# One group of a fused attention and two-layer kernel: its first dense layer by seven products throughout, in a new order of all operations

## The chip, the cores and the metric

The kernel runs on one core of a Trainium2 chip. The metric is device time in microseconds, lower is better. Five engines work side by side, each through its own queue in order: TensorE (PE; PEld are its weight loads), VectorE (DVE), ScalarE (ACT), GpSimd (POOL) and SyncE (SP), which issues DMAs. They wait for each other by semaphores.

## The reference

Attention without a softmax feeds two dense layers:

```
scores = q @ k^T / sqrt(64);  attn = max(scores, 0)^2 / 448
x = (attn @ v), heads side by side: 3584 tokens x 768
h = x @ w_in        (768 x 2048)
g = h * sigmoid(1.702 h)
out = g @ w_out     (2048 x 768)
```

There are 8 batches, 12 heads, 448 positions and 64 dimensions per head. Inputs and output are fp32; the kernel computes in fp16 with fp32 accumulation.

## The kernel before

**Attention.** There are 24 units `u`: a batch and four of its heads. For unit `u` and each of seven blocks `j`, `scores` (word `s`, line 150) gives two tiles of 128x448 by four matmuls of 64x64 weights. `relu` (`r`, lines 161 on VectorE and 163 on ScalarE) takes each out of PSUM, `square` (`x`, line 88 on VectorE or GpSimd, 169 on ScalarE) squares both, and `attn_v` (`a`, line 181) multiplies by `v`, 28 matmuls. `xt_evac` (`e`) brings the result out as columns of `x^T` for a token group.

**Groups.** The tokens form eight groups `g` of 384 and 512 tokens in turn (`gblk = [6, 8] * 4`). Group 1 has 512. The tiles are `xe` and `xo` (x of even and odd groups), `ge` and `go` (the activations).

**First layer.** A group's h has 16 feature blocks of 128. It can be made in two ways. Plainly: `m1` (word `f`, line 228), three words of two matmuls for a block, then gelu (`g`, line 214) from PSUM into a fp32 tile `gf` and `widen` (`v`, line 217), which scales it to fp16 in `ge` or `go`. Or by a unit `i` of four feature blocks at once, with seven products instead of eight over halves of weights, features and tokens: `unit_product` (word `u`, seven words of six matmuls of half the columns, line 203) into two PSUM banks, with `unit_snap` (`t`, three copies out of the first bank), `unit_add` (`b`, three additions of the second bank to a copy), and gelu and widen of four quarters. It uses sums of weights (`S`, of `win` into `winS`) and of x (`T`), made by VectorE once for a unit or a group. There are five `gf` buffers.

**Second layer.** Pairs of 128-token tiles are multiplied by seven products too: `pair_product` (`p`, line 203, eight matmuls), with `A` (sums of activations), `W` (sums of `wout` into `wT`), `h` (`pair_snap`), `l` (`pair_last`). A group of 384 tokens has one tile over, done by `single` (`i`, evacuated by `n`). `o` and `q` store.

**Loads.** `jk`, `jq`, `V` (k, q, v of a unit), `jwa`, `jwb` (halves of a `win` block) and `jo` (a quarter of `wout`) are DMAs with a cast, issued by GpSimd, and so in one queue with its widenings. `Lk`, `Lq` are plain fp32 loads by SyncE, cast by `K` and `Q` on any engine and transposed by `Rk`, `Rq` (DMA) or, for the first six units, `tk`, `tq` on TensorE with `ek`, `eq`. `G3` makes SyncE wait until `win` block 3 has landed. `I` makes the identity matrix, `z` are matmuls on zeros.

**The order.** One list of words, written out by hand in the file, is gone through from first to last; each word issues its operation on its engine, so an engine's queue is the words for it in that order. A word is name, numbers, `:engine` (a, d or p for ScalarE, VectorE, GpSimd) and `@` PSUM banks. `u1.3.2` is group 1, unit 3, product 2 (counted from 0). Before the change group 1 makes its blocks 0 to 7 with `m1` and its units 2 and 3 by products; groups 2 to 7 are by products, group 0 by `m1`.

Of the kernel before, what the change touches and what calls it, by code (L numbers as in the profile page):

```python
# [15 lines left out]
def kernel(  # L16
# [406 lines left out]
    with tc.manual_schedule():  # L423
# [35 lines left out]
        def zeros(e, p, n):  # L459
# [8 lines left out]
            "jq1 z13@0 Lk0 I K0:d tk0@1 ek0 z1 Lq0 Q0:a tq0@2 tq1@3 jk1 eq0 s0.1@4.5 jwb2 jk2 "  # L468
            "s0.6@6.7 s0.4@0.1 r0.4.0:d r0.6.0 tk1@2 ek1 jq2 jq3 eq1 s0.3@6.0 r0.1.1 r0.4.1 "
            "r0.1.0 x0.1 s0.0@5.2 r0.0.0 s0.2@1.4 r0.2.0:d r0.3.1:d r0.3.0 s0.5@3.5 r0.6.1 "  # L470
            "s1.1@6.1 r0.2.1 r0.0.1:d s1.2@7.0 s1.5@4.2 x0.0 r0.5.0 r1.1.1 r1.2.1 jk3 x0.4 "
            "r0.5.1:d tq2@3 r1.2.0 x0.2 x0.6:a x0.5 x0.3 V0 r1.5.1 s1.0@1.0 x1.2 tk2@7 r1.5.0:d "
            "r1.0.0 ek2 tk3@5 r1.0.1 jwa0 s1.3@2.1 eq2 r1.1.0 x1.1:a V2 a0@0.6 V1 x1.5:a r1.3.1 "
            "s1.4@4.7 ek3 r1.3.0 jq4 jwb0 s2.1@3.5 r1.4.1 e0.0.1 s2.2@1.2 r1.4.0:d jk4 e0.0.0 "
            "jwa2 s1.6@4.7 x1.3 r1.6.1:d r2.1.0 r2.2.1 tq3@3 r2.2.0 e0.1.0 x1.4 r1.6.0 x1.6 "
            "r2.1.1 x1.0:p s2.6@2.1 jwa1 x2.2 s2.0@7.0 r2.0.1 r2.0.0 a1@4.5 r2.6.1 jwb1 e0.1.1:a "
            "e1.0.0:a s2.5@0.7 s2.3@1.6 r2.3.0 r2.3.1 e1.1.0:a x2.1 eq3 r2.6.0:d e1.0.1:a "
            "s2.4@3.2 r2.5.0:d r2.4.0:d r2.4.1:d jk5 f0.3.0@1 r2.5.1:d f0.2.0@0 x2.0:p tq4@6 eq4 "
            "tk4@4 s3.3@3.2 x2.6:p x2.3:a e1.1.1:a x2.4:p s3.2@7.5 x2.5:a jq5 r3.2.1:d r3.3.1:d "
            "r3.3.0 r3.2.0 f0.3.1 V3 ek4 f0.2.1 f0.0.0@6 s3.0@5.3 a2@2.7 e2.0.0 r3.0.0 S2.1 "  # L480
            "r3.0.1 x3.0:a e2.0.1:a s3.1@4.5 r3.1.0 f0.1.0@3 f0.0.1 f0.1.1 f0.1.2 e2.1.0:a g0.1 "
            "f0.0.2 V4 V5 jwb3 f0.2.2 x3.2 jwa3 g0.0 r3.1.1:d g0.2 f0.3.2 g0.3 x3.3 e2.1.1 "
            "s3.4@4.2 s3.5@5.3 r3.4.1:d s3.6@6.7 f0.8.0@0 f0.8.1 f0.4.0@1 G3 v0.1 r3.5.1:d r3.5.0 "
            "r3.4.0 x3.4 x3.5 x3.1 f0.8.2 f0.4.1 f0.4.2 r3.6.1 g0.8 s4.1@2.5 r3.6.0 v0.3 r4.1.1:d "
            "s4.3@3.4 r4.1.0 s4.2@7.0 r4.2.1 g0.4 f0.6.0@6 f0.6.1 f0.6.2 r4.2.0:d x3.6 tq5@2 "
            "tk5@5 r4.3.0 r4.3.1 x4.3 g0.6 x4.2:a x4.1 ek5 s4.0@0.7 a3@1.3 r4.0.1 r4.0.0 v0.0 "
            "s4.6@4.6 s4.4@7.5 jo0.0 eq5 f0.10.0@0 r4.4.0:d f0.10.1 f0.10.2 x4.0 v0.8 e3.0.0:a "
            "r4.6.1:d r4.4.1 f0.7.0@2 s5.4@1.7 e3.0.1:a s4.5@5.3 r4.6.0 g0.10 s5.1@4.6 v0.10 "
            "r4.5.0 f0.5.0@0 f0.5.1 f0.5.2 x4.6 f0.11.0@5 f0.11.1 f0.11.2 v0.6 f0.7.1 r4.5.1 "
            "r5.4.1 r5.1.0:d r5.1.1:d g0.5 x4.5:a v0.5 f0.7.2 r5.4.0:d s5.0@4.3 x4.4 s5.2@7.6 "  # L490
            "a4@0.1 r5.0.0:d r5.0.1:d g0.7 g0.11 jo0.1 v0.11 s5.6@2.5 r5.2.1 r5.2.0 s5.5@4.6 "
            "s5.3@3.7 r5.6.0:d e4.0.1:a f0.9.0@1 r5.3.1:d r5.3.0 r5.5.1:d v0.7 S0.1 r5.6.1:d "
            "f0.15.0@2 f0.15.1 r5.5.0 f0.14.0@3 x5.6 f1.1.0@7 jo1.1 f0.14.1 x5.5 v0.4 x5.1:a "
            "f0.9.1 v0.2 S3.1 jo1.0 f0.9.2 g0.9 v0.9 f0.13.0@4 f0.13.1 f0.12.0@6 f0.12.1 f1.3.0@5 "
            "e4.0.0:a S2.2 x5.4 Lq6 f0.15.2 Lk6 x5.0:a x5.3:a S2.3 S1.1 x5.2 f1.7.0@1 f0.14.2 "
            "g0.14 f0.12.2 g0.15 g0.12 S3.2 f1.7.1 f0.13.2 f1.5.0@0 Q6:d f1.0.0@3 f1.1.1 S2.4 "
            "g0.13 v0.13 a5@2.6 v0.15 e5.0.0 K6 e5.0.1:a Lk7 v0.14 S1.2 f1.0.1 f1.5.1 T1.1 "
            "f1.4.0@4 T1.2 v0.12 f1.7.2 S3.3 T1.4 W2.1 W0.1 f1.5.2 g1.7 v1.7 f1.6.0@2 A0.0.1@0 "
            "Lq8 g1.5 W3.1 f1.4.1 f1.4.2 g1.4 W2.2 f1.0.2 g1.0 Rk6 Rq6 v1.5 v1.0 f1.6.1 f1.3.1 "
            "u1.2.0@6 f1.2.0@1 t1.2.0 f1.1.2 W1.1 f1.3.2 K7 Rk7 u1.3.0@0 u1.2.1@4 g1.3 g1.1 v1.1 "  # L500
            "v1.3 Q8:a v1.4 f1.6.2 f1.2.1 f1.2.2 g1.2 v1.2 p0.0.0@3 h0.0.0 V8 b1.2.1 t1.3.0:d "
            "u1.3.2 u1.2.2 u1.2.3 Lk8 V6 W2.4 W0.2 T1.3 W2.3 g1.2.1 g1.6 t1.2.2 K8:p s6.0@5.7 "
            "s6.2@1.2 v1.2.1 r6.0.0 W1.2 u1.2.4 W3.2 r6.2.1:d r6.0.1 r6.2.0 t1.2.4 x6.0:a W3.3 "
            "u1.3.1@5 p0.0.1@2 W3.4 b1.3.1 A0.0.2@1 Lq7 s6.1@7.1 u1.2.5 b1.2.3 r6.1.1 r6.1.0:d "
            "l0.0.1 u1.3.3 u1.2.6 s6.3@1.7 W0.4 x6.1:a p0.0.2 W1.3 b1.2.6 Rq8 g1.2.3 r6.3.0:d "
            "t1.3.2 s6.5@4.1 A0.0.4 h0.0.2:d r6.3.1 u1.3.4 W0.3 v1.2.3 p0.0.3 Q7:a v1.6 r6.5.0 "
            "s6.6@7.4 Lq9 Q9 r6.5.1 g1.3.1 g1.2.5 t1.3.4 x6.2:a S3.4 A0.0.3 x6.5:a r6.6.0 W1.4 "
            "v1.3.1 b1.3.3 x6.3 V7 s6.4@1.6 r6.4.0 p0.0.4 u1.3.6 h0.0.4:d u1.3.5 Rq7 r6.6.1 "
            "l0.0.3 r6.4.1:d b1.3.6 p0.0.5 g1.2.6 g1.3.5 s7.4@7.1 s7.0@4.6 g1.3.6 g1.3.3 v1.3.3 "
            "l0.0.5:a v1.3.6 x6.6 s7.2@5.0 r7.2.0 Lk9 x6.4 r7.4.1:d r7.4.0 p0.0.6 r7.2.1 r7.0.0:d "  # L510
            "Rk8 K9:p r7.0.1:d l0.0.6 v1.2.6 x7.0:a s7.1@3.1 r7.1.1 r7.1.0:d a6@5.4 e6.0.0 "
            "e6.0.1:a e6.1.1 Lk11 e6.1.0 s7.5@7.6 s7.3@0.2 r7.5.1:d p1.0.0@3 A0.2.5@1 r7.5.0 x7.1 "
            "r7.3.0 s8.0@1.4 x7.4 s7.6@5.7 r7.6.1:d r8.0.0:d s8.1@0.6 v1.2.5 v1.3.5 r7.3.1 x7.3:a "
            "i0.2.0@2 K11:p r8.1.1 r7.6.0 x7.2 Lq10 x7.5:a x7.6 S1.3 r8.0.1 S0.3 s8.2@6.7 "
            "r8.2.0:d r8.1.0 a7@5.1 s8.3@4.0 o0.1 e7.0.1 Rk9 Rq9 x8.1 r8.3.0:d x8.0 n0.2.0:a "
            "Q10:a r8.2.1 e7.1.1 A1.0.1@0 s8.6@2.6 x8.2:a r8.3.1 i0.2.1@7 r8.6.0 r8.6.1 x8.3:a "
            "h1.0.0 V11 s8.5@0.4 e7.0.0 r8.5.0 x8.6 s8.4@2.1 r8.4.0 r8.4.1 A1.0.2@1 r8.5.1:d "
            "p1.0.1@6 n0.2.1:a x8.4 p1.0.2 e7.1.0:a Lk10 s9.0@0.2 s9.1@1.4 r9.0.0:d r9.1.1:d "
            "l1.0.1 x8.5:a r9.0.1 r9.1.0 a8@7.5 s9.3@2.0 S1.4 x9.0 r9.3.0:d e8.0.0:a K10:p "
            "e8.0.1:a A1.0.4 T2.1 s9.2@1.4 p1.0.3 Rq10 S0.2 r9.2.1 h1.0.2 r9.2.0 r9.3.1 e8.1.0:a "  # L520
            "e8.1.1:a u2.1.0@4 u2.0.0@2 t2.0.0 t2.1.0 u2.0.1@1 s9.4@0.7 u2.1.1@5 Lq11 T2.2 r9.4.0 "
            "b2.0.1 x9.3 u2.1.2 u2.0.2 u2.2.0@0 T2.4 Q11:a b2.1.1 T2.3 g2.0.1 A1.0.3 u2.0.3 "
            "t2.0.2 Rk11 u2.0.4 t2.0.4:d o0.0 g2.1.1 t2.1.2 Rk10 b2.0.3 Lq12 r9.4.1 v2.1.1 u2.1.3 "
            "u2.1.4 Lk12 u2.0.5 t2.2.0 u2.2.1@7 S0.4 v2.0.1 u2.0.6 t2.1.4 x9.1:a b2.1.3 u2.1.6 "
            "b2.2.1 g2.0.3 g2.2.1 u2.2.2 v2.2.1 v2.0.3 b2.0.6 g2.0.6 g2.0.5 v2.0.6 b2.1.6 g2.1.3 "
            "Rq11 u2.1.5 t2.2.2:d v2.1.3 g2.1.5 v2.1.5 u2.2.3 u2.3.0@1 g2.1.6 u2.3.1@5 u2.2.4 "
            "v2.0.5 s9.5@2.4 t2.3.0:d b2.3.1 v2.1.6 u2.3.2 V9 t2.2.4 o0.2 b2.2.3 Q12:a t2.3.2 "
            "A1.2.1@0 A1.2.2@1 g2.3.1 u2.2.5 v2.3.1 u2.3.3 g2.2.3 u2.2.6 r9.5.1 u2.3.4 p1.0.4 "
            "t2.3.4:d u2.3.5 r9.5.0:d b2.2.6 g2.2.5 K12 Lq14 h1.0.4 Lk13 v2.2.3 g2.2.6 g2.3.5 "
            "s10.1@4.0 x9.2 r10.1.1 A1.2.3 x9.4:a l1.0.3 s9.6@2.7 p1.0.5 b2.3.3 s10.0@1.0 u2.3.6 "  # L530
            "v2.2.6 r9.6.0:d r9.6.1 r10.0.0 r10.1.0:d Rk12 V13 b2.3.6 x9.6:a r10.0.1:d Rq12 "
            "p1.2.0@2 g2.3.6 l1.0.5:a x9.5 p1.0.6 l1.0.6 h1.2.0 s10.3@7.4 g2.3.3 s10.2@1.5 Q14 "
            "r10.2.1 r10.2.0 r10.3.0:d a9@0.3 s10.6@6.5 s10.4@7.1 r10.6.0:d x10.0:a r10.6.1:d "
            "p1.2.2 r10.4.1:d e9.0.0:a e9.0.1 x10.1:a v2.3.5 h1.2.2 o1.1 p1.2.1@6 x10.2:a x10.6 "
            "s10.5@0.5 l1.2.1 s11.1@1.3 r10.3.1 r10.5.0:d r10.4.0 x10.4:a x10.3:a r11.1.0:d "
            "p1.2.4 r10.5.1:d r11.1.1:d p1.2.3 s11.0@4.7 s11.3@0.1 v2.2.5 x10.5 h1.2.4 r11.0.0:d "
            "V10 v2.3.6 a10@5.3 r11.3.1 r11.3.0 s11.2@4.1 e10.0.1:a r11.0.1:d l1.2.3 A1.2.4 "
            "v2.3.3 e10.0.0:a Lq13 Q13 K13:p s11.6@7.0 r11.6.0 p1.2.5 x11.1:a o1.0 r11.6.1:d "
            "r11.2.1:d r11.2.0 p1.2.6 A2.0.1@0 s11.5@3.5 s12.3@0.7 x11.0:a s11.4@1.4 l1.2.5:d "
# [135 lines left out]
```

## Time and profile before

| | |
|---|---|
| runs (3) | median 369.36 us, 368.82 to 371.6 |
| profiled execution | span 372.2 us from its first to its last instruction; the page gives no other time of it |
| busy: PE, DVE, ACT, POOL | 358.6, 302.9, 281.3, 137.6 us |
| granted TensorE clock, mean | 0.987 |
| read from HBM, written | 45.61 MB, 11.01 MB |
| first layer by `m1`, group 1 | 48 matmuls of 512 columns |

A group of instructions is printed as line, engine, operation, output<-input, shapes, count, then busy time and mean ns of one, then the idle time before them and what ended it. Durations of neighbours overlap, so the time that one adds is read from start to start. In the slices each digit is a fortieth of the span. The chain of waits is followed back from the last instruction.

### The profile page before, as it was taken

What the parts mean: (1) busy time and instruction counts of PE and PEld (TensorE: products, weight loads), DVE (VectorE), ACT (ScalarE), POOL (GpSimd) and SP (SyncE); (2) the same over time, 40 slices, a digit from 0 to 9 for tenths busy, and PEclk for the clock granted to TensorE, in tenths of its full rate; (3) what the DMA queues carried; (4) which work ended last, traced back from release to release, by engine and by line L of the source; (5) the groups of instructions that cost most, each with busy time, mean ns of one, the idle gap of its engine ahead of it and who ended that gap; (6) DMA issues with size and microseconds to landing.
All of it is one profiled execution on the core that took longest, in us unless ns stands there. A gap on an engine that the chain in (4) does not pass through costs nothing.

```text
span 372.2 us, 9025 instructions
## 1 busy us (share of the span) xinstructions
PE 358.6 (96%) x3562; PEld 233.2 (63%) x3562; DVE 302.9 (81%) x556; ACT 281.3 (76%) x540; POOL 137.6 (37%) x202
## 2 busy tenths in 40 slices
PE   7699999799999999999999999999999999999994
PEld 4345554465559755786558755686559755688562
DVE  3988995899988989877998889898897899856552
ACT  3979985579989998798897898868887889346210
POOL 5859264714412732054411613344602421034300
PEclk9989999899999999999999999999999999999998
DMA  9999999918997791849965695784583242300334
GB/s 192 183 204 163 213 209 226 218 18 173 200 225 165 151 221 25 167 105 174 179 170 98 146 184 172 188 171 119 82 205 23 41 97 26 85 2 2 85 97 117
DMA packets 65226, 51.38 MB, mean 138 GB/s; under 512 B 35744, under 2 KB 61856, under 8 KB 65184
## 3 DMA queue, kind: packets, MB, share of 16 engines
q1 hardware_dynamic: 48176, 36.22, 43.2%
q0 software_dynamic: 16608, 14.09, 26.4%
q8 instruction: 28, 0.46, 0.5%
q10 hardware_dynamic: 400, 0.49, 0.4%
q14 instruction: 14, 0.11, 0.1%
HBM read 45.61 MB, written 11.01 MB: 152 GB/s over the span
## 4 chain that ended last, share of the span: by engine, by line
PE 84%; DMA 7%; DVE 3%; POOL 2%; ACT 1%; issue 1%; SPq 0%; DVEq 0%; ACTq 0%
PE ox L203 30%; PE hx L203 27%; PE sc L150 9%; PE av L181 8%; PE os L203 6%; DMA wout<-in_moe_w_out_dram 4%; PE ht L228 3%; DMA v<-in_v_dram 2%; DMA qst<-in_q_dram 1%; DVE wT L88 1%; PE tr L131 1%; POOL ge L217 1%; DVE at L88 1%; ACT gf L214 1%; POOL go L217 0%
## 5 line engine op out<-in xcount | busy, mean ns | idle before, releaser
L163 ACT ACTIVATE at<-sc 128x448 f16<-128x448 f32 x201 | 99.6, 559 | 13.0 <-PE sc L150 12.7
L161 DVE TENSOR_SCALAR at<-sc 128x448 f16<-128x448 f32 x135 | 79.8, 618 | 10.9 <-PE sc L150 10.6
L217 POOL TENSOR_SCALAR go<-gf 128x512 f16<-128x512 f32 x64 | 42.6, 665 | 79.1 <-ACT gf L214 75.7
L169 ACT ACTIVATE at<-at 128x896 f16<-128x896 f16 x72 | 68.2, 962 | 1.7 <-DVE at L161 1.2
L217 POOL TENSOR_SCALAR ge<-gf 128x384 f16<-128x384 f32 x64 | 35.4, 554 | 74.0 <-ACT gf L214 70.8
L203 PEld LDWEIGHTS <-win 128*128 128x128 f16 x624 | 56.7, 98 | 8.5 <-issue 2.4
L88 DVE TENSOR_TENSOR at<-at 128x896 f16<-128x896 f16 x92 | 55.9, 631 | 1.7 <-ACT at L163 0.6
L88 DVE TENSOR_TENSOR gf<-hx,gf 128x512 f32<-128x512 f32 (+1 forms) x78 | 47.7, 625 | 11.5 <-ACT gf L79 5.4
L150 PE MATMUL sc<-qT,kT 64*64 64x448 f16 x672 | 52.6, 363 | 1.3 <-DVE qT L83 0.6
L214 ACT ACTIVATE gf<-gf 128x512 f32<-128x512 f32 (+1 forms) x78 | 43.8, 585 | 11.7 <-DVE gf L88 11.6
L203 PEld LDWEIGHTS <-winS 128*128 128x128 f16 x468 | 43.4, 99 | 8.2 <-issue 3.9
L203 PE MATMUL ox<-wout,go 128*128 128x384 f16 x256 | 46.4, 326 | 0.0
L203 PEld LDWEIGHTS <-go 128*128 128x128 f16 x320 | 29.9, 98 | 23.2 <-issue 5.8
L203 PE MATMUL hx<-T,winS 128*128 128x256 f16 (+1 forms) x312 | 38.2, 268 | 2.7 <-DVE gf L83 2.7
L181 PE MATMUL av<-at,v 64*64 64x448 f16 x672 | 37.5, 357 | 1.0 <-DMA v<-in_v_dram 1.0
L203 PEld LDWEIGHTS <-ge 128*128 128x128 f16 x256 | 24.0, 98 | 18.4 <-issue 4.1
L150 PEld LDWEIGHTS <-kT 64*64 64x64 f16 x672 | 18.7, 106 | 26.3 <-issue 22.1
L79 ACT ACTIVATE gf<-hx 128x384 f32<-128x384 f32 (+1 forms) x44 | 23.3, 537 | 15.4 <-PE hx L203 12.0
L203 PE MATMUL ox<-wT,asum 128*128 128x384 f16 x192 | 34.9, 327 | 0.0
L203 PE MATMUL hx<-xo,win 128*128 128x256 f16 x252 | 31.4, 273 | 0.4 <-ACT gf L79 0.4
L203 PEld LDWEIGHTS <-asum 128*128 128x128 f16 x224 | 21.1, 98 | 16.3 <-issue 3.3
L81 ACT ACTIVATE osb<-ox 128x384 f32<-128x384 f32 x32 | 15.4, 496 | 19.2 <-PE ox L203 19.1
(75 smaller groups left out, 475.9 us busy)
## 6 DMA issues: line engine op xcount, KB each, us to landing
out_dram<-osb SPq DMA_DIRECT2D x52, 192.0 KB, 3.2
kst<-in_k_dram SPq DMA_DIRECT2D x19, 448.0 KB, 4.7
qst<-in_q_dram SPq DMA_DIRECT2D x19, 448.0 KB, 4.9
v<-in_v_dram POOLq DMA_DIRECT2D x24, 224.0 KB, 5.6
win<-in_moe_w_in_dram POOLq DMA_DIRECT2D x8, 384.0 KB, 9.7
wout<-in_moe_w_out_dram POOLq DMA_DIRECT2D x4, 768.0 KB, 11.5
q<-in_q_dram POOLq DMA_DIRECT2D x5, 224.0 KB, 5.6
k<-in_k_dram POOLq DMA_DIRECT2D x5, 224.0 KB, 6.5
```

The costliest lines, as they stand in the source:

```text
L79: nc.scalar.activation(out=o, in_=i, func=AF.Copy)
L81: nc.scalar.activation(out=o, in_=i, func=AF.Copy, scale=scale)
L88: eng[e].tensor_tensor(out=o, in0=x, in1=y, op=op)
L150: nc.tensor.matmul(out=sc[a][c, 0:S], lhsT=st["kT"][r, j, c], rhs=st["qT"][r, :, c], start=True, stop=True)
L161: nc.vector.tensor_scalar(out=o, in0=i, scalar1=0.0, scalar2=None, op0=ALU.max)
L163: nc.scalar.activation(out=o, in_=i, func=AF.Relu)
L169: nc.scalar.activation(out=at, in_=at, func=AF.Square)
L181: nc.tensor.matmul(out=av[s][64 * a:64 * a + 64, 0:S], lhsT=v16[r, a, 64 * j:64 * j + 64], rhs=at[r, a, :], start=(j == 0), stop=(j == J - 1))
L203: nc.tensor.matmul(out=o, lhsT=lhs(i), rhs=rhs(i), start=start and i == 0, stop=i == n - 1, skip_group_check=True)
L214: nc.scalar.activation(out=o, in_=i, func=AF.Gelu_apprx_sigmoid, scale=1.0 / SC)
L217: eng[e].tensor_scalar(out=o, in0=i, scalar1=SC, scalar2=1.0, op0=ALU.mult, op1=ALU.mult)
L228: nc.tensor.matmul(out=hp[g, f][:, 0:n], lhsT=w[:, i, fo:fo + 128], rhs=xts[g][:, i, 0:n], start=i == 0, stop=i == NK - 1)
```

## The change

Group 1's blocks 0 to 7 are now units 0 and 1 by seven products. Out go 24 words `f1.0.0` to `f1.7.2`, 8 gelus and 8 widens; in come 14 words `u1.0.*`, `u1.1.*`, 6 `t1`, 6 `b1`, 8 gelus and 8 widens. The numbers of `S`, `T`, `A` and `W` stay. The whole list is reordered, the PSUM banks are given out anew, and many operations change engine:

| operation | before | after |
|---|---|---|
| widen `v` | GpSimd 128 | GpSimd 96, VectorE 32 |
| square `x` | ScalarE 72, VectorE 92, GpSimd 4 | ScalarE 59, VectorE 109, GpSimd 0 |
| relu `r` | ScalarE 201, VectorE 135 | ScalarE 227, VectorE 109 |
| casts `K`, `Q` | ScalarE 16, VectorE 4, GpSimd 18 | ScalarE 5, VectorE 7, GpSimd 26 |
| snapshot `t` | ScalarE 44, VectorE 34 | ScalarE 53, VectorE 31 |
| `pair_last` `l` | ScalarE 8, VectorE 40 | ScalarE 0, VectorE 48 |
| `e`, `ek`, `eq` | ScalarE 40, VectorE 44 | ScalarE 45, VectorE 39 |

The four `jo` words come before the first widen. Only the list changes, no function. Its parts that the text speaks of:

```diff
-            "jq1 z13@0 Lk0 I K0:d tk0@1 ek0 z1 Lq0 Q0:a tq0@2 tq1@3 jk1 eq0 s0.1@4.5 jwb2 jk2 "
...
-            "s3.4@4.2 s3.5@5.3 r3.4.1:d s3.6@6.7 f0.8.0@0 f0.8.1 f0.4.0@1 G3 v0.1 r3.5.1:d r3.5.0 "
...
-            "s4.6@4.6 s4.4@7.5 jo0.0 eq5 f0.10.0@0 r4.4.0:d f0.10.1 f0.10.2 x4.0 v0.8 e3.0.0:a "
...
-            "a4@0.1 r5.0.0:d r5.0.1:d g0.7 g0.11 jo0.1 v0.11 s5.6@2.5 r5.2.1 r5.2.0 s5.5@4.6 "
...
-            "f0.15.0@2 f0.15.1 r5.5.0 f0.14.0@3 x5.6 f1.1.0@7 jo1.1 f0.14.1 x5.5 v0.4 x5.1:a "
-            "f0.9.1 v0.2 S3.1 jo1.0 f0.9.2 g0.9 v0.9 f0.13.0@4 f0.13.1 f0.12.0@6 f0.12.1 f1.3.0@5 "
...
-            "f1.4.0@4 T1.2 v0.12 f1.7.2 S3.3 T1.4 W2.1 W0.1 f1.5.2 g1.7 v1.7 f1.6.0@2 A0.0.1@0 "
-            "Lq8 g1.5 W3.1 f1.4.1 f1.4.2 g1.4 W2.2 f1.0.2 g1.0 Rk6 Rq6 v1.5 v1.0 f1.6.1 f1.3.1 "
-            "u1.2.0@6 f1.2.0@1 t1.2.0 f1.1.2 W1.1 f1.3.2 K7 Rk7 u1.3.0@0 u1.2.1@4 g1.3 g1.1 v1.1 "
-            "v1.3 Q8:a v1.4 f1.6.2 f1.2.1 f1.2.2 g1.2 v1.2 p0.0.0@3 h0.0.0 V8 b1.2.1 t1.3.0:d "
-            "u1.3.2 u1.2.2 u1.2.3 Lk8 V6 W2.4 W0.2 T1.3 W2.3 g1.2.1 g1.6 t1.2.2 K8:p s6.0@5.7 "
...
-            "q7.2.0.0 p7.0.6 h7.2.4 l7.2.3 q7.3.1.0:a q7.2.0.1:a l7.0.6 o7.0 p7.2.5 l7.2.5:d "
-            "q7.3.0.0:a q7.3.0.1 q7.3.1.1:a p7.2.6 l7.2.6 q7.2.1.0:a q7.2.1.1"
+            "Lk0 z13@0 z1 Lq0 jq1 jk1 jwb2 Q0:a I K0:p tk0@1 ek0 tq0@2 eq0 jk3 tq1@3 s0.1@4.5 "
+            "s0.2@6.7 eq1 s0.0@0.1 r0.1.1 jq2 r0.2.1 s0.5@2.3 r0.1.0:d V0 r0.2.0:d r0.5.0 r0.0.0 "
...
+            "s2.2@3.5 r2.2.1 r2.2.0 r2.0.1 x1.5 x1.3 x1.6 eq3 r2.3.1 a1@4.1 V3 jwb3 s2.6@5.3 "
+            "r2.1.1:d e1.1.0 e1.0.0:a r2.6.1 r2.6.0:d e1.0.1:a jwa3 V4 f0.3.0@6 V5 s3.0@2.0 "
+            "r3.0.0:d s3.2@7.4 jo1.0 e1.1.1 s2.4@3.5 r2.4.1:d f0.3.1 jo0.0 r3.2.0 r2.4.0:d x2.0:a "
+            "s2.5@2.1 x2.1 s3.3@5.7 r3.2.1 f0.2.0@3 f0.2.1 r2.5.0:d jo1.1 r2.5.1 tq4@4 x2.2 tk4@2 "
+            "r3.3.0 x2.4 x2.3:a x2.6:a x2.5 a2@1.5 jo0.1 ek4 r3.3.1 r3.0.1 eq4 e2.1.0:a s3.1@2.7 "
...
+            "g0.3 S1.1 s4.1@7.0 r3.4.0 x3.4 s4.2@6.5 r3.5.1 g0.8 g0.1 x3.5 g0.4 r4.2.0 s4.3@3.1 "
...
+            "T1.3 u1.1.0@7 u1.0.1@4 K6 S2.4 Lk7 t1.1.0 T1.2 u1.1.1@1 b1.0.1 Lq8 u1.0.2 S3.3 Rk6 "
+            "u1.1.2 S2.3 T1.4 f0.15.2 t1.0.2 u1.0.4 g1.0.1 v1.0.1 f0.13.2 Rq6 u1.0.3 S0.4 b1.1.1 "
+            "W3.1 g0.15 v0.15:d S1.3 t1.1.2 g1.1.1 g0.13 v0.13:d t1.0.4 f0.12.0@6 f0.12.1 f0.12.2 "
...
+            "A0.0.1@0 g1.0.6 u1.3.1@3 u1.1.6 W0.2 K7 g1.1.3 b1.1.6 u1.2.2 t1.2.2 p0.0.0@5 W1.3 Lk8 "
...
+            "p7.2.6 q7.3.1.0 l7.0.6 l7.2.5 q7.3.1.1:a q7.3.0.1:a o7.0 q7.3.0.0 l7.2.6 q7.2.1.1:a "
+            "q7.2.1.0"
```

## The prediction, made before the changed kernel ran

> **What bounds the kernel now.** I read the page's busy rows and slices, the chain of waits in order of time, the windows around its one break, and the timeline there. First the page.
>
> ```profile
> PE 358.6 (96%) x3562; PEld 233.2 (63%) x3562; DVE 302.9 (81%) x556; ACT 281.3 (76%) x540; POOL 137.6 (37%) x202
> PE   7699999799999999999999999999999999999994
> ...
> PEclk9989999899999999999999999999999999999998
> DMA  9999999918997791849965695784583242300334
> ```
>
> TensorE is the bound from about 30 us to the end, with a slow start and one dent (slice 7, 65 to 74 us), where its clock falls too. DMA is full up to that dent. The chain of waits there, start and length first:
>
> ```profile
> 51.51 14.72 DMA wout<-in_moe_w_out_dram
> 67.27 0.63 DVE asum L88
> 68.29 2.72 DVE wT L88 x3
> 71.01 0.60 DVE gf L88
> 71.61 0.61 DVE gf L83
> 72.26 3.75 PE hx L203 x18
> ```
>
> The last `wout` load lands at 66.2. VectorE stood idle for it, because the weight sums (`wT`, words `W`) lie in its queue ahead of the addition and snapshot (`gf`) that the next seven-product matmuls need. The timeline gives both waits:
>
> ```profile
> 66.32 1.03 DVE L88 TENSOR_TENSOR wT<-wout,wout 128x768 f16<-128x768 f16 x2 [3.85 <-DMA wout<-in_moe_w_out_dram]
> ...
> 72.26 3.75 PE L203 MATMUL hx<-T,winS 128*128 128x256 f16 x18 [2.71 <-DVE gf L83]
> ```
>
> The windows (us, then busy PE, PEld, DVE, ACT, POOL, the clock, DMA share, GB/s) show the aftermath: half clock for 3.7 us.
>
> ```profile
> 72.30:76.00 3.70, 3.70 (x22) 2.43 (x25) 3.70 (x6) 1.06 (x2) 1.96 (x2) 0.54 0.95 155
> ...
> 0.00:30.00 30.00, 24.40 (x316) 12.90 (x316) 21.66 (x42) 21.73 (x44) 20.45 (x28) 0.94 1.13 194
> 30.00:69.00 39.00, 38.92 (x375) 21.65 (x375) 31.13 (x56) 31.89 (x63) 21.39 (x33) 1.00 1.18 198
> ```
>
> **What the skill says.** "VectorE: DVE Perf Modes", section on the perf-mode tier table: a tensor_scalar on fp32 in SBUF runs at two elements per cycle. "SBUF — State Buffer", section "SBUF: two separate sides": VectorE and GpSimd share one port pair; a VectorE instruction of that mode, or with two SBUF inputs, and a GpSimd instruction exclude each other. The trace agrees: the same sum of 128x1024 halves takes
>
> ```profile
> L88 DVE TENSOR_TENSOR asum<-ge 128x1024 f16<-128x1024 f16 x8 | 6.5, 812 | 0.5 <-POOL ge L217 0.5
> ...
> L88 DVE TENSOR_TENSOR asum<-go 128x1024 f16<-128x1024 f16 x8 | 5.5, 682 | 0.0
> ```
>
> and the slow ones are those with a GpSimd operation beside them. "Perfetto Trace Analysis", section on the SWDGE DMA instruction, says that a GpSimd load may generate more descriptors than fit in the descriptor buffer; no load of this trace shows GpSimd held by it (issues take 0.70 to 0.94 us).
>
> **The change, part by part.**
>
> *Products.* Out go 8 blocks x 6 = 48 matmuls of 512 columns, in come 2 units x 7 x 6 = 84 of 256. Durations on the page overlap; what counts is start to start:
>
> ```profile
> 58.78 4.92 PE L228 MATMUL ht<-xo,win 128*128 128x512 f16 x22
> ...
> 238.49 17.03 PE hx L203 x156
> ```
>
> (4.92 - 0.38 of the last one) / 21 = 0.216 us, and 17.03 / 156 = 0.109 us. "TensorE: Matmul & The Clock Gate", section "Back-to-back issue gap", states N/2.4 + 2.5 ns, that is 216 and 109: it agrees. 48 x 0.216 - 84 x 0.109 = 10.37 - 9.16 = **-1.2 us** of TensorE. Small: one product in eight saved, one sixteenth of the groups' work touched.
>
> *Switches.* The new order leaves the scores for full-size matmuls 58 times (59 before) and returns 54 times (57). A switch pair costs about 0.26 us (a product of 8 takes 1.41 before scores and 1.30 elsewhere in the chain; the step out of scores is some 0.16 longer than within): **-0.3 us**, as an estimate.
>
> *The broken chain.* All four `wout` loads stood on GpSimd's queue among the widenings `v0.x`; the last was issued at 51.51. In the new order they come before the first widening, behind `V5`, which waits for `a1` (about 24 us here). DMA gives 194 to 198 GB/s and is full. Loads up to unit 5, `win` and `wout` are 10.9 MB as written, units 6's `k` and `q` 0.9 more, so all has landed near 11.8 / 0.197 = 60 us, the first two `wout` blocks near 51. VectorE's first `W` (`W3.1`) stands behind 48.9 us of its own work and at least 8.3 us of idle start, so after 57 us. The wait of 3.85 us is gone, with it TensorE's 2.71 and the half clock: 18 matmuls in 3.75 us where 18 x 0.109 = 1.96 is normal, 1.8 lost. Sum **-4.5 us**. I take it whole; at worst a later `W` waits again.
>
> *More on VectorE, earlier.* Added are 6 additions (686 ns each) and 6 snapshots (598 on ScalarE), no operation goes (gelu, widen, `S` and `T` are as many as before). Engines change too: 32 widenings and 4 squares leave GpSimd; VectorE gets 32 widenings, 17 squares (631), 8 more `pair_last` and three casts, and gives 26 relus (618) to ScalarE, which gives 13 squares (962) and 11 casts away. GpSimd gets 8 casts. A widening on VectorE is not in the trace. The cast of 896 fp32 elements from SBUF took 614 ns; at two per cycle (0.96 GHz by the page) 512 elements take 0.2 us less: 0.41. At one per cycle it would be the snapshot's 0.687. I take 0.41, which is 0.34 start to start. Start to start (relu 0.53, square 0.53, addition 0.60, sums 0.47 to 0.60) VectorE's list sums to 295 us, from 285. That is below TensorE's 340, so over the whole run it is covered. It is not at the front. Counted to `p0.0.0`, VectorE's work ahead of it is 56.0 us, was 49.8; TensorE's is 54.7, was 55.2. The list's last VectorE operand for `a5` stands 2.9 us deeper in its queue than `a5` in TensorE's (below 0 before), for `u1.0.2` 1.6, for `a6` 0.9, and from group 2 on it is ahead again.
>
> To price it: `a5` began at 57.33 with 44.6 us of TensorE work ahead, so 12.7 were lost till then. In the new order 40.0 + 12.7 = 52.7 by TensorE; by VectorE 42.9 + 8.3 (idle in the first 30 us) + between 0 and 3.6 (its idle from 30 to 57) = 51.2 to 54.8. So 0 to 2.1 us there, and up to 2 more to `a6` from the port pair, whose two users are both busy. From both sides 0 to 4; I take **+1.5 us**.
>
> *No square on GpSimd.* Four of 1800 ns held its queue, and `jq5`, from 20.5 to 30 us in the loads. With DMA full it gains nothing more; below nothing is excluded, as VectorE's four (0.53 each) are counted.
>
> *Start and end.* `K0` is cast on GpSimd (about 1.0 against 0.63 us), but `Q0` on ScalarE (5.42 + 0.95) ends later and still decides. At the end `o7.0` is stored some 0.5 us nearer to the last product, beside the last stores: 0 to +0.5, I take **+0.2**.
>
> Sum: -1.2 - 0.3 - 4.5 + 1.5 + 0.2 = -4.3 on the profiled span of 372.2, so 367.9. The runs' median is 369.36 and their highest 371.6: the profiled run is at the slow end, and a part of its dent may be missing in the others. By ratio 369.36 x 367.9 / 372.2 = 365.1; for that doubt I take half a microsecond less gain: **365.6**.
>
> **Rivals.**
> 1. *VectorE binds the front, and eats the gain.* For: slices of 9.6 to 9.9 tenths on VectorE after 80 us, and 6 us more of it before `p0.0.0`. Against: TensorE's fixed switch losses give it time back. Widenings at 0.69 instead of 0.41 (8 of them before `a8`: 2.2 us) and port conflicts at 0.25 each (812 against 682, and more for the slow half) on some 8 (2.0) add 4.2: 367.9 + 4.2 = 372.1, by ratio 369.3.
> 2. *GpSimd is held at the loads; slower.* At 20.5 us some 2.1 MB were issued and not landed, at 51.5 us 1.9 MB: the most that the trace shows. The new order has issued 10.9 MB by about 30 us, when 5.8 have landed: 5.1 MB. If the descriptor buffer holds less, GpSimd stands at a `jo` word and the widenings behind it wait; after five gelus the `gf` buffers are full, ScalarE stops and TensorE with it. Down to 2.1 MB takes 3.0 / 0.197 = 15 us, to 45 us. `g0.4`, the sixth, is due near 37 (29 us of VectorE's list and 8.3 idle): 8 us lost and half clock 1.8 more. It decides from a hold of over 7 us. 367.9 + 9.8 = 377.7, or 374.8.
> 3. *More is won.* VectorE's front costs nothing and `V0`, issued 2 us earlier, ends the wait of 1.0 us before `a0` with a part of the half clock after it: -1.5 - 1.5, 362.6.
>
> That the change isn't what it says is excluded by the lists: 48 matmuls out, 84 in, no `x` with `:p`.
>
> **Numbers.** Forecast 0.50 (its own range 364 to 368), rival 1 0.25, rival 2 0.13, rival 3 0.12. One per cent, 3.7 us, is about what a measurement here tells from no change. Faster by more: 0.38 of the forecast and rival 3: 0.50. Slower by more: rival 2 and a sliver of rival 1: 0.16. Within: 0.34. Range 362 to 372.
>
> **What will show it.** TensorE without a wait over 1 us between 60 and 80 us and full clock there; `wout` landed by 60; `a6` near 88 (92.6 before); VectorE above 95% from 40 to 90 us; widenings on VectorE near 0.42 us. I am wrong if GpSimd shows a load issue of over 2 us near 30, if TensorE waits for VectorE by more than 2 us in sum before `a8`, or if the gain appears after 100 us, where I see none.

## The result, and the profile after

| | median | lowest to highest | runs | ratio to before, 95% interval |
|---|---|---|---|---|
| before | 371.25 us | 368.41 to 374.97 | 20 | |
| after | 369.01 us | 368.05 to 371.57 | 20 | 0.9956, 0.9931 to 0.9980 |

The forecast was 365.6 us, 1.0% faster; measured is 0.44%. Measured twice more, the ratio was 0.9971 (0.9947 to 0.9995) and 0.9982 (0.9954 to 1.0010). So the change is worth 1 or 2 us of a typical execution, not the four that the prediction saw. The ratios compare fast runs alone, leaving out those over 1.5% above the fastest of their kernel, and so are not the quotients of the medians.

The profiled pair says something else. Each run lists its time and its span, and the time is 1.8 us longer. The profiled execution of before (span 372.2) was thus one of 374.0 us, near the top of its runs; that of after (span 366.7, 368.49 us) lies in the lower half of its own. Between these two lie 5.5 us, between the medians 2.2.

The page after:

```profile
PE 357.0 (97%) x3598; PEld 236.7 (65%) x3598; DVE 314.2 (86%) x586; ACT 278.4 (76%) x550; POOL 119.8 (33%) x174
PE   8889999999999999999999999999999999999995
...
PEclk9899999999999999999999999999999999999999
DMA  9999999299899699744993488635790122111124
```

Slice 7 is whole and its clock full: the dent is gone. A half clock remains at 13.6 to 17.0 us. VectorE's timeline where the first weight sums (`wT<-wout`) stood idle for 3.85 us before:

```profile
59.04 0.68 DVE L88 TENSOR_TENSOR gf<-hx,gf 128x512 f32<-128x512 f32 x1
59.64 0.55 DVE L88 TENSOR_TENSOR wT<-wout,wout 128x768 f16<-128x768 f16 x1
60.10 0.35 DVE L217 TENSOR_SCALAR ge<-gf 128x384 f16<-128x384 f32 x1
```

The first sum starts at 59.64 with no bracket behind it, that is without a wait. The windows (us, then busy PE, PEld, DVE, ACT, POOL, clock, DMA share, GB/s):

```profile
30.00:60.00 30.00, 29.63 (x325) 18.36 (x321) 29.16 (x57) 27.82 (x60) 10.66 (x15) 1.00 1.25 223
60.00:70.00 10.00, 10.00 (x86) 8.20 (x84) 9.48 (x20) 8.10 (x16) 3.17 (x5) 1.00 0.51 113
70.00:80.00 10.00, 10.00 (x84) 6.23 (x83) 10.00 (x18) 8.60 (x17) 6.37 (x8) 1.00 0.70 144
```

TensorE is full, and so is VectorE. To see what limits each stretch, I take the start of a word on TensorE less the TensorE work listed ahead of it, priced start to start (0.216 us a matmul of 512 columns, 0.109 of 256, and so on, the same prices for every kernel). What is left is time lost, the start and the switches included:

| lost before | before | before, profiled again | after | after, profiled again |
|---|---|---|---|---|
| `a2` | 11.6 | 10.9 | 10.4 | 8.9 |
| `a5` | 12.7 | 12.0 | 12.6 | 13.1 |
| `a6` | 18.4 | 14.8 | 13.8 | 14.3 |
| `a10` | 20.2 | 16.7 | 16.9 | 17.4 |
| `p7.2.6` | 25.8 | 22.4 | 21.8 | 22.3 |

The work ahead of `p7.2.6` is 340.2 us before and 339.0 after: the seven products' 1.2 us are there. Two things stand out. Before, the loss from `a5` to `a6` is 5.7 us in one execution and 2.8 in the next of the same program. After, the second execution is 1.5 us ahead at `a2` and half a microsecond behind at `a5`: something between holds it. The experiments take these in turn.

### The profile page after: what moved, and what is told of

Read it like the earlier page. It is cut to its first block, busy times and chain, and to the rows that moved or that the text cites. A ratio compares the mean times of both kernels' runs of the same rounds, so it can differ in the third digit from the quotient of the medians.

```text
span 366.7 us, 9109 instructions
## 1 busy us (share of the span) xinstructions
PE 357.0 (97%) x3598; PEld 236.7 (65%) x3598; DVE 314.2 (86%) x586; ACT 278.4 (76%) x550; POOL 119.8 (33%) x174
## 4 chain that ended last, share of the span: by engine, by line
PE 88%; DVE 7%; ACT 3%; issue 1%; DVEq 0%
PE hx L203 32%; PE ox L203 29%; PE sc L150 9%; PE av L181 7%; PE os L203 6%; PE ht L228 4%; DVE at L88 2%; ACT at L163 2%; DVE at L161 2%; PE zp L463 1%; PE tr L131 1%; ACT at L169 1%; DVE go L88 0%; DVE winS L88 0%; DVE kT L83 0%
## 5 line engine op out<-in xcount | busy, mean ns | idle before, releaser
L163 ACT ACTIVATE at<-sc 128x448 f16<-128x448 f32 x227 | 112.8, 562 | 19.0 <-PE sc L150 18.5
L161 DVE TENSOR_SCALAR at<-sc 128x448 f16<-128x448 f32 x109 | 64.7, 615 | 6.0 <-PE sc L150 5.2
L88 DVE TENSOR_TENSOR at<-at 128x896 f16<-128x896 f16 x109 | 68.2, 649 | 1.5 <-ACT at L163 0.9
L203 PEld LDWEIGHTS <-win 128*128 128x128 f16 x672 | 61.4, 98 | 8.2 <-issue 1.7
L217 POOL TENSOR_SCALAR go<-gf 128x512 f16<-128x512 f32 x47 | 30.9, 657 | 84.1 <-ACT gf L214 82.4
L169 ACT ACTIVATE at<-at 128x896 f16<-128x896 f16 x59 | 56.4, 964 | 1.0 <-DVE at L161 0.7
L217 POOL TENSOR_SCALAR ge<-gf 128x384 f16<-128x384 f32 x49 | 27.6, 564 | 64.8 <-ACT gf L214 63.1
L203 PEld LDWEIGHTS <-go 128*128 128x128 f16 x320 | 30.2, 98 | 22.3 <-issue 4.4
L79 ACT ACTIVATE gf<-hx 128x512 f32<-128x512 f32 (+1 forms) x53 | 28.6, 545 | 12.4 <-PE hx L203 10.3
L203 PE MATMUL hx<-xo,win 128*128 128x256 f16 x288 | 35.9, 273 | 0.0
L181 PEld LDWEIGHTS <-v 64*64 64x64 f16 x672 | 20.4, 108 | 14.0 <-issue 4.0
```

What stands on the lines that cost most here:

```text
L79: nc.scalar.activation(out=o, in_=i, func=AF.Copy)
L88: eng[e].tensor_tensor(out=o, in0=x, in1=y, op=op)
L161: nc.vector.tensor_scalar(out=o, in0=i, scalar1=0.0, scalar2=None, op0=ALU.max)
L163: nc.scalar.activation(out=o, in_=i, func=AF.Relu)
L169: nc.scalar.activation(out=at, in_=at, func=AF.Square)
L181: nc.tensor.matmul(out=av[s][64 * a:64 * a + 64, 0:S], lhsT=v16[r, a, 64 * j:64 * j + 64], rhs=at[r, a, :], start=(j == 0), stop=(j == J - 1))
```

## Experiments

Edits are moves of words in the list. Ratios are to the kernel before, run beside them.

### The dent: is it always there, and what removes it?

**Before, once more.** 

> The kernel before, unchanged, for more executions of it and a second profile. Theory A (the dent at 70 us is a race between the last wout load and VectorE's weight sums, so its size differs from execution to execution, and the first profile showed a large one): times spread over 4 us or more as before (368.4 to 375), the quick ones with a mean clock near 1.0 and the slow ones with 0.98 to 0.99, and this profile's wait of the weight sums for wout differs from 3.85 us by over 1 us. Theory B (the dent is there in every execution, and the new order gives its gain back elsewhere): the wait is 3.85 us within half a microsecond and the clock does not go with the time.

Measured: 369.20 us (368.41 to 373.22, 14 runs), 0.9981 (0.9947 to 1.0015); its profiled execution took 370.56. VectorE still waits for the last `wout` load, but less:

```profile
63.82 1.03 DVE L88 TENSOR_TENSOR wT<-wout,wout 128x768 f16<-128x768 f16 x2 [2.00 <-DMA wout<-in_moe_w_out_dram]
```

TensorE's matmuls with `T` and `winS`, which stood 2.71 us before, have no bracket now:

```profile
68.64 2.13 PE L203 MATMUL hx<-T,winS 128*128 128x256 f16 x18
```

The page has the half clock of the start, and none in slice 7:

```profile
PEclk9989999999999999999999999999999999999999
```

In the first profile the wait ended at 66.32, 2.5 us later. Here 2.0 us of VectorE's wait stop TensorE not at all; there 3.85 us stopped it for 2.71, and 3.4 us of half clock followed. So the dent has a threshold somewhere between, and in these two executions the arrival of the last load falls on either side of it.

**Loads early, in the old order.**

```diff
-... jwa3 g0.0 ...  v0.0 ... jo0.0 ... g0.11 jo0.1 v0.11 ... jo1.1 ... v0.2 S3.1 jo1.0 ...
+... jwa3 jo1.0 jo0.0 jo1.1 jo0.1 g0.0 ...  v0.0 ... g0.11 v0.11 ... v0.2 S3.1 ...
```

> The order before with one thing changed: the four wout loads are issued right behind the last win load, ahead of the first widening. No product, no engine changes. Theory A: the dent is gone, the times draw together near the kernel before's quick ones, 368 to 369.5 us, ratio about 0.994, so as good as the whole change; no wait over 1 us between 60 and 80 us. Theory B: the profile loses 4.5 us but the times do not, ratio 0.998 to 1.002.

Measured: 370.04 us (369.00 to 371.41, 14 runs), 0.9998 (0.9972 to 1.0024). VectorE starts the first sum without a wait:

```profile
62.18 1.43 DVE L88 TENSOR_TENSOR wT<-wout,wout 128x768 f16<-128x768 f16 x2
```

The upper tail is gone (371.41 against 375.06 of the runs beside it), the median has not moved by more than can be told. Of these 14 executions 8 have a mean granted clock of 0.997 or more, and a median of 369.3 us; the other 6 have 370.5. Beside them before has 369.0 (14 executions) and 371.5 (17). So removing the dent alone shortens the long executions and not the quick ones. That is the first error of my sum.

**Sums behind the addition and snapshot, in the old order.**

```diff
-... T1.4 W2.1 W0.1 f1.5.2 ... g1.5 W3.1 f1.4.1 ... g1.4 W2.2 ... t1.2.0 f1.1.2 W1.1 ... b1.2.1 t1.3.0:d u1.3.2 ...
+... T1.4 f1.5.2 ... g1.5 f1.4.1 ... g1.4 ... t1.2.0 f1.1.2 ... b1.2.1 t1.3.0:d W2.1 W0.1 W3.1 W2.2 W1.1 u1.3.2 ...
```

> The order before, loads as they are; the five weight sums that stand in VectorE's queue ahead of the first addition and snapshot of unit 2 and 3 (b1.2.1, t1.3.0) are moved behind them. Theory A, read more closely: the load may land as late as it likes, as only the queue order makes TensorE wait: ratio 0.994 to 0.997, TensorE without the 2.7 us wait at 70 us; a rest is left if later products wait for the sums. If the late load itself binds (products that need wout or its sums), the wait only moves: ratio 0.999 to 1.002.

Measured: 373.30 us (371.91 to 374.28, 10 runs), 1.0084 (1.0053 to 1.0114). The wait has moved instead of going:

```profile
74.89 1.85 PE L203 MATMUL hx<-xo,win 128*128 128x256 f16 x12 [2.45 <-DVE xo L88]
```

The in-place subtraction `T1.3` now stands behind the displaced sums, and the matmuls that read it wait 2.45 us. A miss: it doesn't isolate the wait, but shows how little room the place has.

**Loads late, in the new order.**

```diff
-... s3.2@7.4 jo1.0 ... f0.3.1 jo0.0 ... r2.5.0:d jo1.1 ... a2@1.5 jo0.1 ... v0.2 ... v0.0 ... v0.7 ...
+... s3.2@7.4 ... f0.3.1 ... r2.5.0:d ... a2@1.5 ... v0.2 jo0.0 ... v0.0 jo0.1 ... v0.7 jo1.1 jo1.0 ...
```

> The changed kernel with the four wout loads put back among GpSimd's widenings, so that they are issued near 36, 46, 50 and 51 us, as before the change. Theory A: the dent comes back in the new order, and larger, as VectorE has no slack there: its first weight sum, due at 59.6, waits till about 66; TensorE waits 3 to 6 us and runs 3.4 us at half clock; ratio to the kernel before 1.00 to 1.01, so 2 to 6 us slower than the changed kernel. Theory B: no slower than the changed kernel by over 0.3%.

Measured: 375.65 us (374.15 to 376.99, 6 runs), 1.0150 (1.0107 to 1.0193), 6.6 above the 369.01 of the changed kernel's first measurement (it did not run beside this one). Two waits, first VectorE's, then TensorE's:

```profile
64.73 0.56 DVE L88 TENSOR_TENSOR wT<-wout,wout 128x768 f16<-128x768 f16 x1 [6.60 <-DMA wout<-in_moe_w_out_dram]
```

```profile
66.25 1.44 PE L203 MATMUL hx<-T,win 128*128 128x256 f16 x6 [5.83 <-ACT gf L79]
```

So a late load still stops VectorE at the sum and TensorE behind it, and the new order needs its loads early. The links between are others than in the order before: ScalarE's snapshot, for which TensorE waits, itself waited 6.42 us for a widening on VectorE, which stood behind the sum.

### After: what holds it between a2 and a5?

**After, once more.** 

> The changed kernel once more, unaltered, to see how its executions spread beside those of the kernel before. Theory A (the only lasting gain is that the stall of the weight sums no longer comes, which the kernel before shows in a part of its executions): median 369.0 within 0.5, few executions over 371; among executions whose mean granted clock is 0.997 or more, the two kernels agree within 0.4 us. Theory B (the changed kernel is faster in every execution, by its smaller TensorE work): 1.2 us or more below the kernel before among those executions too.

Measured: 369.42 us (367.81 to 371.45, 22 runs), 0.9971 (0.9947 to 0.9995). The profile has full clock throughout and an early `a2` (27.30, was 28.73), but `a5` at 53.04 (was 52.53). GpSimd's timeline:

```profile
30.53 0.70 POOL L104 DMA_DIRECT2D v<-in_v_dram  x1 [1.27 <-DMA win<-in_moe_w_in_dram]
32.28 1.77 POOL L415 DMA_DIRECT2D wout<-in_moe_w_out_dram  x2 [1.05 <-DMA win<-in_moe_w_in_dram]
35.17 0.87 POOL L415 DMA_DIRECT2D wout<-in_moe_w_out_dram  x1 [1.12 <-DMA q<-in_q_dram]
36.38 0.87 POOL L415 DMA_DIRECT2D wout<-in_moe_w_out_dram  x1 [0.34 <-DMA v<-in_v_dram]
37.33 0.54 POOL L217 TENSOR_SCALAR ge<-gf 128x384 f16<-128x384 f32 x1
```

ScalarE's:

```profile
34.80 0.94 ACT L214 ACTIVATE gf<-ht 128x384 f32<-128x384 f32 x2
37.91 0.49 ACT L214 ACTIVATE gf<-ht 128x384 f32<-128x384 f32 x1 [2.17 <-POOL ge L217]
```

TensorE's:

```profile
38.45 0.58 PE L131 MATMUL tr<-ident,q 128*64 128x128 f16 x14 [1.53 <-ACT gf L214]
```

Read in order: each load's issue waits for an earlier load to land (by the trace's semaphore numbers the one eight before it on GpSimd), so with DMA full the four `wout` issues are spread to 36.38. The first widening stands behind them in GpSimd's queue and starts at 37.33. Five gelus have filled the five `gf` buffers; the sixth, `g0.4`, waits 2.17 us. Its input holds PSUM bank 2, which the transposes `tq5` need: TensorE waits 1.53. The profile with the late start shows no such wait; it is 1.5 us later at `a2`. What the better start wins is lost again here.

**VectorE relieved.** Eight widenings go back to GpSimd:

```diff
-... v0.6:d ... v0.10:d ... v0.11:d ... v0.15:d ... v0.13:d ... v1.1.1:d ... v1.0.5:d ... v1.1.6:d ...
+... v0.6 ... v0.10 ... v0.11 ... v0.15 ... v0.13 ... v1.1.1 ... v1.0.5 ... v1.1.6 ...
```

> The changed kernel with the eight widenings that VectorE does before the sixth unit's attention is through put back on GpSimd (v0.6, v0.10, v0.11, v0.15, v0.13, v1.1.1, v1.0.5, v1.1.6). VectorE has 8 x 0.34 = 2.7 us less in front. If VectorE binds the front: 0.7 to 2 us faster than the changed kernel, and TensorE loses that much less before the seventh unit's attention. If not: equal within 0.4 us. If GpSimd's slower widenings keep the activation buffers longer, or block VectorE on the shared port: up to 1 us slower.

Measured: 369.19 us (367.98 to 370.80, 22 runs), 0.9966 (0.9945 to 0.9988): 0.2 below the changed kernel beside it, within the spread. From `a5` to `a6` it loses 1.2 us, as the changed kernel does. These widenings on VectorE do not bind the front.

**All 32 widenings back on GpSimd** (the same edit for every `v` with `:d`). 

> The changed kernel with all 32 widenings that VectorE does put back on GpSimd. If VectorE's list is covered after the front, as the prediction has it, this equals the kernel with eight put back within 0.4 us. If VectorE's load matters all along: a further 0.5 to 1.5 us faster. If widening late on GpSimd delays the second layer's operands: 0.5 to 3 us slower.

Measured: 369.28 us (368.44 to 371.16, 22 runs), 0.9968 (0.9947 to 0.9989). Equal again: the move of the widenings is worth nothing either way, on GpSimd 141.9 us busy instead of 120.2. In the profiles of these two versions ScalarE's wait for the first widening is 1.4 and 0.8 us instead of 2.17, though up to that place GpSimd's list is the same: the hold too differs from execution to execution.

**Group 1's first blocks plainly, in the new order.**

```diff
-... u1.0.0@3 f0.13.1 ... T1.3 u1.1.0@7 u1.0.1@4 ... u1.0.6 W0.1 v1.0.3 u1.2.1@0 ...
+... f1.0.0@3 f0.13.1 ... f1.0.1 f1.0.2 f1.1.0@7 g1.0 ... f1.7.2 v1.6:d g1.7 T1.3 W0.1 u1.2.1@0 ...
```

> The changed order, but group 1's first eight feature blocks made plainly again: 48 matmuls of 512 columns in the places of the 84 of 256; the 6 additions and 6 snapshots of those units are gone, the in-place sums of x and of the first two weight blocks stand behind the last plain matmul. TensorE has 1.2 us more, VectorE 3.6 us less before the 80th us. If TensorE's work is the bound there, the time is 1.2 us above the changed kernel (ratio to it 1.003). If VectorE is the bound in front and eats the saving, it is equal within 0.5 us or lower.

Measured: 373.37 us (372.57 to 375.72, 10 runs), 1.0094 (1.0060 to 1.0127), 4.0 above the changed kernel, more than either theory gave. By the account of lost time, 1.2 of it is TensorE's work and 2.9 are new losses of the places that I gave the words, for instance

```profile
63.48 1.14 PE L228 MATMUL ht<-xe,win 128*128 128x384 f16 x6 [0.69 <-ACT gf L214]
```

So it cannot price the products alone. It shows only that these places lose more than the products save.

### The hold taken away

**Two widenings ahead of the last two loads.**

```diff
-... r2.5.0:d jo1.1 r2.5.1 ... a2@1.5 jo0.1 ek4 ... e2.1.1 g0.0 S0.1 ... f0.3.2 v0.2 f0.8.0@1 ... v0.0 s4.6@0.4 ...
+... r2.5.0:d r2.5.1 ... a2@1.5 ek4 ... e2.1.1 g0.0 v0.2 v0.0 jo1.1 jo0.1 S0.1 ... f0.3.2 f0.8.0@1 ... s4.6@0.4 ...
```

> The changed kernel with the last two wout loads (jo1.1, jo0.1) moved behind the first two widenings (v0.2, v0.0) in GpSimd's queue. Theory C (in front the changed order is held by GpSimd: its first widening stands behind four loads whose issues wait for earlier loads, so that the five gf buffers fill up, ScalarE stops at the sixth gelu and TensorE at tq5): ScalarE's wait for the widening (2.2 us at 36 us in the last profile of the changed kernel) and TensorE's 1.5 us go; a5 starts 1 to 2 us earlier than its 52.5 to 53.0; median 0.5 to 1.5 us below the changed kernel, near 368.2. Theory D (the loads themselves are the limit there, whatever the queue): a5 stays at 52.5 or later, median as the changed kernel's within 0.4.

Measured: 367.58 us (366.29 to 369.78, 9 runs), 0.9904 (0.9868 to 0.9941). GpSimd's timeline:

```profile
32.58 1.77 POOL L415 DMA_DIRECT2D wout<-in_moe_w_out_dram  x2 [0.83 <-DMA win<-in_moe_w_in_dram]
34.42 1.64 POOL L217 TENSOR_SCALAR ge<-gf 128x384 f16<-128x384 f32 x2
36.12 1.81 POOL L415 DMA_DIRECT2D wout<-in_moe_w_out_dram  x2
```

The widenings fit where the queue stood waiting for loads anyway: the last two issues follow at once, without a wait. This profile has a late start (`a2` at 28.77), so its `a5` (52.25) shows little of it; the two versions below have early ones.

**The same two widenings on VectorE, the loads untouched.**

```diff
-... f0.1.2 f0.3.2 v0.2 f0.8.0@1 ... f0.4.2 g0.3 S1.1 ... r3.5.1 g0.8 g0.1 ... v0.0 s4.6@0.4 ...
+... f0.1.2 f0.3.2 f0.8.0@1 ... f0.4.2 v0.2:d g0.3 S1.1 ... r3.5.1 v0.0:d g0.8 g0.1 ... s4.6@0.4 ...
```

> The changed kernel with its first two widenings (v0.2, v0.0) on VectorE instead, the loads as they were. If GpSimd's queue is the cause (C), ScalarE's wait goes as in the kernel before this one in the list, and a5 comes 0.5 to 1.5 us earlier, less VectorE's 0.7 us. If VectorE binds the front, 0.5 us slower than the changed kernel. If the loads are the limit (D), the same within 0.4.

Measured: 367.98 us (367.57 to 369.13, 6 runs), 0.9901 (0.9863 to 0.9939). GpSimd still issues its last `wout` load at 36.01 and widens from 36.97, but ScalarE's wait is gone, `tq5` starts at 36.88 instead of 38.45 and `a5` at 51.01:

```profile
36.88 0.58 PE L131 MATMUL tr<-ident,q 128*64 128x128 f16 x14
```

The loads are the same, so they were not the limit: the queue was. Both edits also bring `v0.0` forward, which stood behind five other widenings and so kept a `gf` buffer longer. That is not the cause: *Loads late, in the new order* leaves the widenings in their places and only takes the loads away from ahead of them, and its profile has no wait at `tq5` either (37.03) and `a5` at 50.95.

**The widenings ahead of the last two loads, and the eight back on GpSimd.** (The first edit of this part with that of *VectorE relieved*.) 

> Both at once: the last two wout loads behind the first two widenings, and the eight widenings of VectorE in front back on GpSimd. The best of the versions if both the queue hold and VectorE's load count in front: 368.0 or below, against 369.0 to 369.4 of the changed kernel. If only the hold counts, equal to the version with that alone within 0.3 us.

Measured: 367.70 us (366.94 to 368.32, 6 runs), 0.9894 (0.9854 to 0.9935). ScalarE's waits between 30 and 42 us, first of the changed kernel (second profile), then of this one (waited for, us in all, times, longest):

```profile
ACT gf L214 <- POOL ge L217: 2.2, 1, 2.2
ACT at L163 <- PE sc L150: 0.5, 1, 0.5
ACT gf L214 <- PE ht L228: 0.2, 1, 0.2
```

```profile
ACT at L163 <- PE sc L150: 0.5, 1, 0.5
ACT gf L214 <- PE ht L228: 0.2, 1, 0.2
```

`a5` starts at 50.85. The three versions agree within their spreads, as they should if only the hold counts.

**After, beside these.** 

> The changed kernel unaltered, on the same chip as the three versions of it, to compare with: median 369.0 to 369.5; in its profile a2 begins between 27.3 and 28.8 us, and a5 between 52.5 and 53.1 whichever it is.

Measured: 369.61 us (368.21 to 373.16, 22 runs), 0.9982 (0.9954 to 1.0010), `a2` at 27.23 and `a5` at 53.33, a little past what was expected, with the same 2.17 and 1.5 us of waiting. The versions without the hold are 1.6 to 2.0 us faster than it, and beat both kernels.

## Why the prediction was right or wrong

**What the executions have in common, and what not.** Each run lists its mean granted clock. A half clock of 3.4 us takes 3.4 x 0.5 / 372 = 0.005 off the mean, so an execution at 0.997 or more had no such stretch (none has 0.996). Of the 124 executions of before that ran beside the experiments, 52 are of that kind, with a median of 368.90 us; the other 72 have 371.86. Of 64 executions of the changed kernel 47 are, with 369.14; the other 17 have 371.24. So where nothing disturbs it the changed kernel is no faster at all (by 0.24 us slower, less than can be told), and what the medians show is that it is disturbed in 27% of its executions instead of 58% (52% without the 15 longest, which the ratios leave out). No profile caught an execution of before with full clock, so what its start looks like is not shown.

Two half clocks take 0.009, so an execution with both lies at 0.991 or lower: of the 72, 21 do. In all four profiles of the old order one half clock is at the start; the second, which two of them have, is the dent's. If that holds for the others, the dent with its half clock was in at most 21 of 124 executions, 17%. It can be fewer: with the loads early in the old order, without a dent in the profile, two of 14 executions have 0.988.

**Products**, -1.2: right as TensorE's work. It stands in the work ahead of `p7.2.6`. In the time a gain of that size appears once the hold is gone: 367.4 to 368.0 in the undisturbed executions of the three versions without it, against 368.9. But they differ from before in the whole order too, and the one run that took the products back could not price them alone, so that the gain is the products' is argued and not shown. On the price, "it agrees" says too much: the section "Back-to-back issue gap" of "TensorE: Matmul & The Clock Gate" in the Trainium skill gives the formula for an isolated matmul, and for a stream a lower figure, about 131 ns at 512 columns. Here a stream of them takes 216 ns each, and the trace decides.

**The broken chain**, -4.5: the mechanism was right, and every mark of it came. The first sum waits for nothing, TensorE has no wait and full clock from 60 to 80, `a6` came at 86.6 where I wrote near 88. The term was mis-sized, and this is the step that failed. I took the dent of one profiled execution "whole", noted that this execution was at the slow end, and then scaled its sum by a ratio to the median, with half a microsecond taken off "for that doubt". That median, 369.36 of three runs, is itself near the 368.90 of executions without a half clock: I took a dent off a time that had hardly one in it. The runs show that a second profile of the same kernel has no dent, that removing the dent in the old order leaves the median at 370.04, and that two executions in five have no half clock to lose. For those the term is 0; for the median of before's 124 executions (370.90 us) it is 2 at most, and the start's half clock is in that. Counted at its share, in at most 21 of 124 executions, the term is 4.5 x 21 / 124 = 0.8 us as a mean, an estimate. Against its own execution the sum was close: 374.0 less 4.3 is 369.7, and the profiled run after took 368.5.

**More on VectorE, earlier**, +1.5, and rival 1: wrong in the cause. VectorE is as full as expected (29.16 of 30 us between 30 and 60), and a widening on it costs what I took (0.35 us for 384 elements, 0.42 for 512 with no GpSimd operation beside it), yet taking eight or all of them away gains nothing that can be measured, nor does it with the hold gone (367.70 against 367.58). The loss is there, of 2.2 to 4.5 us between `a2` and `a5` against 1.1 before, but not these widenings'. Without the hold 1.7 to 2.1 are left, and what they are stays open. Two numbers came out by luck: rival 1's 369.3 is near the measured 369.01, and the terms other than the chain sum to +0.2, as undisturbed executions differ by +0.24. But +1.5 stands there for another cause, and the better start is not in it.

**Rival 2**, GpSimd held at the loads: its chain was right link by link (a held issue, widenings behind it, five full `gf` buffers, ScalarE, TensorE), and its size and cause were not. I looked for a full descriptor buffer and a hold to 45 us; it is the wait of an issue for an earlier load to land, and it holds the first widening to 37.3 us. That costs 1.6 to 2.0 us by the medians, not 8. Of the three profiles of the changed kernel the two with a good start show it. In the late-starting one it does not appear: that page alone would have hidden it. My test, a load issue of over 2 us, could not see it either: the issues take 0.87 (in the profile before 0.66 to 0.94, where I wrote from 0.70), the time is in the waits between them.

**Start and end**, +0.2, and rival 3: the start was better than I said. All four profiles of the old order have a half clock that begins between 15.9 and 18 us; of the ten of the new order and its versions two have one, at 13.6 and 13.7. With that half clock `a2` starts at 28.7 in the changed kernel, in the four of the old order at 29.6 to 30.7; with full clock at 27.2 and 27.3. I left this gain to rival 3. Why the new start is disturbed less often was not tried; TensorE's wait at `tk3`, just ahead of the half clock or at its beginning (1.0 to 2.3 us in the four old ones), is gone in all ten.

*Switches* (-0.3) and *No square on GpSimd* (0) are within what the account of lost time can tell and stay open.

## What to carry to other kernels

Before a stall is priced, ask how often it occurs: one profile of a kernel whose runs spread by 2% is one draw, and a stall with a threshold (a load that lands just too late) is in it or not. Compare the profiled execution's own time with the median first, and count a stall at its share. And when loads are moved ahead on a queue that also computes, price the issues' waits as work of that queue: two widenings put between the loads gave back 2 us, since the queue stood there waiting.

## What the runs showed of the hardware

In these profiles GpSimd's issue of a load takes 0.66 to 0.95 us, and in the new order it can wait 0.2 to 2.2 us before that, each time for the load eight places earlier in its queue. By the trace eight semaphores (99 to 106) tell in turn that a load has landed, and an issue waits for the one that it takes again. So this limit on loads under way lies in the program as it is built; whether the chip would take more at a time was not tried. It shows in the timeline's brackets and not in the length of the issue.

A TensorE wait of 2.71 us was followed by 3.4 us of half clock, and so was the one of 2.45 us with the sums behind. At the start, where TensorE is busy in part only, it came after waits of no more than 1.4 us in three profiles of the old order (2.3 in the fourth) and 0.9 in the first of the changed kernel. The length of the wait alone does not decide it: the other two profiles of the changed kernel have the same wait of 0.87 us near 11 us and full clock.

With the clock halved at the start the program may end no later. In the changed kernel's first measurement the five executions with a half clock have a median of 368.5 us, the other 15 have 369.2; in the profiles of this kernel the hold comes with a full clock alone. But in its other two measurements those with a half clock are slower, by 1.5 and 2.6 us.
